# A delta-rule recurrence feeding a low-rank mixer and an MLP: the first group's product with w1 taken apart and moved into the recurrence

## The chip, the cores and the metric

The kernel runs on one core of one Trainium2 chip. The metric is device time in microseconds (us); the kernel before has a median of 610.22 us over three runs. A core has five engines that run their own instruction streams: PE (TensorE, matmuls; its weight loads are listed apart as PEld), DVE (VectorE), ACT (ScalarE), POOL (GpSimd) and SP (SyncE, which here only issues DMA transfers). SBUF is the on-chip memory of 128 partitions, PSUM the matmul output, 8 banks of 128 x 512 float32. PE's clock is granted by a throttle; the profile shows it as a share of full speed.

## The reference

Two blocks follow each other. The first is a delta-rule attention over B = 4 batches, H = 8 heads, S = 768 tokens, head size D = 48:

```
k_n = k / (|k| + 1e-6)
for t in range(768):                      # per batch and head, state is 48 x 48
    y[t]  = q[t] @ state
    state = state + beta[t] * outer(k_n[t], v[t] - k_n[t] @ state)
```

The eight heads side by side make x, 768 x 384 per batch. The second block mixes tokens by a product of rank 32 and then applies an MLP per token:

```
u   = x + (x.T @ U @ V).T                 # U 768 x 32, V 32 x 768
out = u + relu(u @ w1) @ w2               # w1 384 x 1536, w2 1536 x 384
```

q, k, v and beta are float32. U, V, w1 and w2 come as float64 and are made float32 on the chip.

## The kernel before, in words

**Attention.** Each batch is cut in 12 chunks of 64 tokens, and 6 chunks make a unit, so units 0 and 1 are batch 0, units 2 and 3 batch 1, and so on up to 7. For a unit the kernel loads k, q, v (and kz, a second copy of half of k) into one of two buffers `slot` (`load`, L301, issued on SP and POOL), normalises k, transposes k and q on PE (`grams`, L375), makes the products of k with itself and with q (L398), and inverts a triangular 64 x 64 matrix per chunk and head. The inversion (`blocks`) substitutes inside 32 x 32 blocks (or 16 x 16 ones) on DVE: `gs` (L450), `prod` (L459), `xt` (L460), and then a transpose into `zz` (L464). For units 0 to 2 the 16-blocks are joined into 32-blocks by two small products each, the joins: L503 (x of the block below), an ACT copy, L515, and DVE's add L519. For units 0 and 1 (`lone`) the operands lie alone on 64 partitions: `alone` is a part of the buffer `hs`, `parted` lies in `S1` and `S2`, written by `part` on ACT (L480), and each product uses the two diagonal tiles of 64 x 64, partitions 0 to 63 to rows 0 to 63 and 64 to 127 to 64 to 127. Two more products (L537 to L550) make the 64-blocks, and L619 and L624 prepare a unit for the recurrence.

**Recurrence.** `recur` goes chunk by chunk through a batch: b (product with the state, L673), z = v - b (DVE, L680), the state's increment (L690) and the new state s (DVE, L694). Outputs y are the products L597 and L604; ACT copies them into X (L587). `X` holds x of two batches. Batch 1 can't enter its recurrence before its own preparation is through; units are prepared two ahead.

**Mixer and MLP.** A batch's 768 tokens make three groups of 256. `front(b, i)` makes, for the first group of a batch, the token product `x.T @ U` (L929) and its copy `tt` (L932), then for each group the product with V (L944), adds it to x (L946), transposes u on PE (L960) and copies it (`ut`, L963). It waits for all 12 chunks of x. `wide(b, i)` has six `channels`, one for each pair of 128-wide feature tiles of w1 in `PAIRS`: six products of 128 x 128 by 128 x 256 (L1014), and ACT's relu into `hs` (L984). `add_up` makes sums (L1035, L1042) for the second product, which uses seven products of quarter size in the place of eight (`narrow`, L1102; results added to X by `gather`, L1048). A program on PE runs in a tiling mode: whole array, 64 x 64 quadrants, 32 x 32 tiles, or column strips of 32.

**Weights.** Fourteen slices come in: 0 is U, 1 is V, 2 to 7 the six pairs of w1, 8 to 13 w2. Each is a DMA of float64 into a staging place (L757, two DMAs of 384 KB from SP for a slice), three DVE instructions (L777, L783, L786) and one ACT cast (L763). There are three staging places, given per slice by `where`: 0 lies in the half of `X` that batch 1 will use, 1 is the buffer `wide`, 2 lies in `hs`. A slice waits for the one before it in its place, for the start of the slice before it, for unit 0's joins if it goes to `hs`, and all of them for `seeded`, a marker of unit 0's inversion.

**Order.** Each piece of work is a Python generator that yields one operation at a time. The order of the operations on all engines is one long list of numbers, ORDER; each entry lets one generator go a step further. `need(...)` names what a generator waits for before it is in the list's reach, and `emitted(...)` marks it as issued. Nothing is scheduled at run time: every engine executes its instructions strictly in this order, with waits on semaphores. The number behind a dot picks the PSUM slot: four pairs of banks (`pair`), of which the last is also the two `mix` banks used by the MLP, set aside by `reserve` from a point on. So an instruction that waits holds up all that stands behind it on its engine, and the DMA queues of SP and POOL are such streams too.

Of the kernel before, what the change touches and what calls it, by code (L numbers as in the profile page):

```python
# [14 lines left out]
L = 64  # L15
# [8 lines left out]
def kernel(ctx: ExitStack, tc: tile.TileContext, q: bass.AP, k: bass.AP, v: bass.AP, beta: bass.AP, moe_U: bass.AP, moe_V: bass.AP, moe_w_ch1: bass.AP, moe_w_ch2: bass.AP, out: bass.AP):  # L24
# [28 lines left out]
    1 0 1 0 1 0 1 0 22 1 38 22 38 22 21 22 14.0 21 2 21 37 151 21 20 151 15.1 36 2 36 167 26 166.2 36 167 26  # L53
    37 168.3 166 43 166 166 37 17.0 168 39 168 168 39 19 168 18.1 2 39 169 2.3 24 2 166 37 171.0 2 2 152 12 2
    168 171 43 153 170 12 36 39 29.2 168 166 38 24 12 172.3 166 171 153 24 173 19 3.1 38 24 3 172 174.0 23 3
    19 3 19 23 32.2 174 19 23 174 175 19 153 172 153 19 19 23 122 25 19 174 42 30.1 19 174 25 19 177 19 174 19
    174 178 19 19 179.2 19 19 3 19 33.3 179 184 40 183 35 183.0 181 186 40 179 187 40 41 122 183 179 187 42 41
    34 179 181.1 179 186 179 122 181 183 122 154 27 27 188 154 185.3 40 181 122 12 181.2 185 181 34 122 176.0
    181 155 181 34 155 181 183.1 122 180 122 180 183 189 27 176 34 180 181.2 183 181 185 180 176 181 180 181.3
    183 41 34 181 34 181 183 180 181 41 34 183.2 182 34 5.0 182 34 182 34 182 34 5.1 34 34 183 5 34 34 183 34  # L60
    5 183.3 34 183 182 4.0 183 182 183 4 190.2 34 156 6.1 190 156 190 6.0 194 192 195 4.3 122 6 195 194.2 122
    157 196 4 157 122 6 197.1 196 4.3 198 194 4 4.0 194 197 4 192.3 122 197 197 122 158 194.2 27 200 158 192
    122 122 194 192 159 159 199.0 194 4.1 192.3 4 122 194 201 4.1 122 199 122 192 199 199 194 160 202.2 122
    193 160 194.0 4 203 194 122 192 194 122 193 194.1 193 122 161 194 193 122 161 4.0 204 192 193 192 193 122
    194 192.3 192 191 4 194 122 191 122 192 4.0 191 206.1 4 191 202 205 4.3 191 191 4 52 207.0 202 4.3 202
    192.2 4 122 192 122 162 207 192 162 206 192 4.3 208 7.2 4 122 207 122 206 207 206 7.3 163 163 53 8.0 7 122
    53 7 122 209 4.1 210.2 4 122 4.3 8.1 4 164 164 122 4.3 122 54 8 210 4 53 211 212.3 4.0 210 4 210 122 4.0 8
    213.2 4 165 4.1 165 122 53 4 214 122 4.0 53 54 215.1 4 53 56 213 122 4.0 53 54 213 212 213 4 53 54 216 4.2
    212 212 217.0 54 4 216 4.3 54 215 4 54 218.2 122 215 4.3 215 54 216 219 217 4 46 218 217 122 217 46.1 216
    218 218 122 67 47.3 220 67 221 67 221 222 223.0 67 221 67 66 221 224.2 67 69 223 223 67 66 223 127.1 67 56  # L70
    224 223 224 66 224 51 224 69 66 66 66 69 49.3 127 66 50.0 225 66 62.2 44 55 226 44 123 55 127.1 228 55 44
    227.0 127 55 63.2 51 55 127.1 231 68 227 55 227 68 127 229.2 55 51 68 51 128.0 51 68 229 233 68 51 128 59
    68 233 51 55 229 68 51 59.1 244 51 56 60.0 245 51 68 234 246 51 56 51 51 128.2 51 234 128 51 51 51 235 249
    51 235 44 254 248.1 247.0 253 65 248 251 236 247 248 69 248 255 248 247 236 247 64 247 237 256 255 57 237
    57 257 251.2 64 251 253.1 251 255 253 64 253 238 57 57 238 64 64 64 240 258 64 259 64 240 259 64 259 64
    129.0 261 260 64 251.2 251 64 241 64 251 251 251 241 64 250 250 239 250 262 129 251.1 251 253.2 251 263
    253 64 251.0 251 64 251 242 250 253 253 251 250 253 250 252 242 264 64 252 252 64 252 64 253.1 253 9.2 64
    253 230.0 9 265 252 9.1 230 252 129.2 64 243 129 230 9 267 9.0 266.2 267 9 268q 266 64 266 9.1 64 268 9
    279.0 64 268 9.2 268 9 64 268 64 9.1 280 279 253.2 64 279 253 279 269 64 253 253 64 64 269 64 64 270 282
    64 64 270 9 78 286 271 287 284 288 283 271 288 283 288 283 272 289 285 283 272 285 273 290 285 285 273 275  # L80
    291 292 292 292 293 9.0 286.2 284.1 286 284 283 284 275 285 9 283 286 285 276 294 276 295 277 296 274 277
    297 298 286.1 284.0 298 286 284 265 284 278 284 286 286 299 281.2 9.0 300q 9 9.1 300 9 311.0 300 9.1 300 9
    300 9.1 312 281 9 301q 281 301 9.1 301 311 281 9 301 311 311 301 313.2 314 9.1 302q 9 9.0 302 9 315.1 302
    9.0 302 9 9.0 302 9 313 316 9.0 315 313 9 303 317 313 315 317 315 317 79 9.0 79 303 9 79 79 319 9.2 318.1
    9 232.0 79 80 79 80 9.2 232 304 79 80 232 9 79 80 9.0 80 82 320.2 9 318 80 9.0 318 304 9 72 318 80 80 72.0
    321 322 9.1 305 9 9.0 320 9 323.1 320 320 73.0 323 323 305 325 323 323 326 9.2 328.0 9 327 324.1 327 328
    9.2 307q 327 9 328 9.2 328 324 328 9 307 77 324 9.2 324 307 75.0 9 70 329.1 330 70 9.2 307 9 77 9.0 329
    307 329 9 329 77 9.2 333 9 334 76.0 306 335 81 308q 77 77 81 308 77 299 77 82 332.1 77 308 9.2 82 81 308 9
    77 82 337.0 77 9.2 308 9 77 9.2 332 338 9 339 337 332 77 332 309 337 77 337 92 77 92 70 130.2 77 92 92 77
    92 93 77 331.1 92 95 130 92 93 336.0 340 331 92 93 130.2 77 93 309 77 93 130 85 93 331 310 93 336 341 93  # L90
    336 341 77 81 130.2 95 77 85.1 95 130 342 88.0 77 342 81 343 86.2 77 81 355 89.1 81 77 357 94 131.0 77 359
    94 356.2 77 94 344q 131 356 94 344 77 94 360.1 344 356 94 356 344 77 360 81 356 77 344 77 362 131.0 77 345
    77 131 360 77 77 345 346 367 360 91 364 360 366 346 94 90 365 95 363 347 363 94 365 70 363 347 83 368 83
    370 361.2 365 83 364.0 365 369 366.1 364 90 366 363 348 366 364 90 361 365 348 365 361 363 369 349 371 369
    83 349 90 90 351 372 363 373 90 373 351 90 373 374 90 352 90 350 375 90 364.1 366.0 364 376 366 90 364 352
    366 90 364 90 366 90 10.2 132.1 10 377 10.0 358.2 10 132 10.0 353 90 10 358 358 353 380 90 90 354 381 90
    381 90 90 10.1 132q.0 10 382 379.2 124 132 10.1 90 383 90 124 383 124 10 90 394 378.0 90 10.1 378 379 384q
    10 379 124 378 90 379 10.1 384 10 90 395.0 384 10.2 124 384 10 90 384 90 10.1 396 395 124 385q 395 10 124
    395 90 10.2 385 124 10 124 397.1 90 385 10.0 385 10 90 10.2 90 385 10 398.0 399 90 397 124 10.2 90 397 386
    397 10 386 400 400 405 404 104 10.1 387 10 403 402 403 124 400 403 387 124 403 124 124 401 124 388 124 124  # L100
    124 406.2 10.1 398 10 388 398 407 398 10.1 404.0 10 404 402.1 404 402 406 402 10.0 406 390 10 406 408 106
    401 409 106 401 409 106 390 410 401 409 106 106 105 106 105 391 411 389 106 105 106 105 105 382 391 412
    108 105 401 105 101.1 413 403 414 401 402.0 402 105 404.2 404 404 102.1 402 392 107 402 107 98 404 107 416
    392 417 107 107 108 107 98.0 419 107 419 99.2 420 107 421 108 10.1 422.0 10 403 423.2 108 422 10.1 422 423
    422 393 10 423 422 423 423 425 424.1 10.0 425 426q 10 10.2 426 10 437.0 103 426 10.2 426 10 10.2 426 10 96
    424 438 96 10.2 437 424 427 437 96 437 10 424 103 10.0 415.2 10 103 103 439.1 10.0 415 427 415 10 103 428
    440 103 103 103 10.2 418.0 10 103 10.2 418 428 10 418 96 442 441.2 10.0 429q 443 10 429 443 10.0 103 429
    441 429 441 10 441 443 10.0 103 429 10 444.2 445 103 10.0 439 430 439 103 439 103 430 10 103 103 446 447.1
    10.0 103 431 10 103 10.0 444 103 10 447 444 444 431 103 447 447 103 118 448 133.0 103 118 118 103 118 449
    433q 118 121 103 118 121 449 433 133 118 119 103 118 119 133.2 433 103 119 433 449 119 133 433 111 119 103  # L110
    133q.1 119 450 451 111.0 103 133 119 103 434 452 119 103 121 103 103 103 112.2 453 103 114.1 455 434 460
    459 117 457 458 435 462 456 121 432 456 456 456 464 134.0 458 454.2 134 461.1 454 134q.0 454 461 454 458
    461 435 461 134 116 458 454 436 461 465 109 465 115.0 466 109 466 467 478 120 116 120 467 120 116 120 116
# [316 lines left out]
    def blocks(n):  # L430
# [45 lines left out]
        def part(h):  # L476
            to = parted(h).rearrange('p (r e) t -> p r e t', r=2)
            for y in range(2):
                yield op('act')
                nc.scalar.mul(to[:, :, :, BK * y:BK * y + BK], cut(zn, h), even[:, y:y + 1])  # L480
            emitted(('parted', n, h))
# [695 lines left out]
```

## Time and profile before

| | us |
|---|---|
| runs, three | 608.35, 610.22, 612.16 (median 610.22) |
| profiled execution, its own time | 612.87 |
| its span, first to last instruction | 611.2 |
| PE busy | 570.2 (93% of the span) |
| DVE busy | 388.7 (64%) |
| ACT busy | 232.1 (38%) |
| POOL busy | 97.8 (16%) |
| mean granted PE clock | 0.935 |
| last z of batch 0's recurrence (DVE, L680) | ends 110.9 |
| first transposes of unit 2's grams (PE, L375) | start 111.6 |
| substitution of units 0 to 3 through (DVE, L464) | 33.0, 57.8, 134.3, 178.9 |

How to read it: the profile is one execution. Busy time is that of an engine's own instructions; waits, semaphores and the issuing of DMAs are not counted. A group of instructions is named by its line in the program, engine, operation and operands, "out<-in". A float32 matmul leaves two records, except a transpose by the transposing form, so 36 products of 128 x 256 are 72 records. A share averaged over the span hides stages; the table of stretches gives the busy time in each of them.

### The profile page before, as it was taken

What the parts mean: (1) busy time and instruction counts of PE and PEld (TensorE: products, weight loads), DVE (VectorE), ACT (ScalarE), POOL (GpSimd) and SP (SyncE); (2) the same over time, 40 slices, a digit from 0 to 9 for tenths busy, and PEclk for the clock granted to TensorE, in tenths of its full rate; (3) what the DMA queues carried; (4) which work ended last, traced back from release to release, by engine and by line L of the source; (5) the groups of instructions that cost most, each with busy time, mean ns of one, the idle gap of its engine ahead of it and who ended that gap; (6) DMA issues with size and microseconds to landing.
All of it is one profiled execution on the core that took longest, in us unless ns stands there. A gap on an engine that the chain in (4) does not pass through costs nothing.

```text
span 611.2 us, 24520 instructions
## 1 busy us (share of the span) xinstructions
PE 570.2 (93%) x11070; PEld 485.8 (79%) x11070; DVE 388.7 (64%) x972; ACT 232.1 (38%) x495; POOL 97.8 (16%) x169
## 2 busy tenths in 40 slices
PE   5798975999899999999999999999999999999997
PEld 4688964788889778788979976988879768655997
DVE  4799855899992136999994299989722225132442
ACT  3546674642442335144234532632342231344000
POOL 8311050530101040512004204110010000000000
PEclk9955665799999999999999999999999999999999
DMA  9933658830000060720004305020000000000010
GB/s 146 155 89 116 203 154 174 136 78 8 4 16 1 29 95 3 137 72 17 15 4 97 82 3 96 8 66 3 29 3 2 29 4 1 26 1 1 17 36 27
DMA packets 63849, 33.34 MB, mean 55 GB/s; under 512 B 50816, under 2 KB 61824, under 8 KB 63744
## 3 DMA queue, kind: packets, MB, share of 16 engines
q1 hardware_dynamic: 56800, 23.21, 17.7%
q0 software_dynamic: 5344, 8.27, 6.3%
q8 instruction: 87, 1.43, 1.0%
q10 hardware_dynamic: 1600, 0.30, 0.3%
q14 instruction: 18, 0.15, 0.1%
HBM read 27.03 MB, written 4.72 MB: 52 GB/s over the span
## 4 chain that ended last, share of the span: by engine, by line
PE 63%; DVE 27%; issue 4%; ACT 3%; DMA 3%; ACTq 0%; DVEq 0%; SPq 0%
PE P L1102 21%; PE P L1014 10%; PE P L201 8%; PE P L838 7%; DVE xt L460 6%; DVE prod L459 6%; PE P L398 3%; PE P L375 2%; DMA wide<-in_moe_w_ch_dram 2%; PE P L604 1%; DVE gs L450 1%; PE P L649 1%; PE P L597 1%; DVE slot L417 1%; PE P L690 1%
## 5 line engine op out<-in xcount | busy, mean ns | idle before, releaser
L1014 PE MATMUL P<-ut,w_sb 128*128 128x256 f32 x456 | 106.3, 385 | 0.8 <-ACT hs L984 0.6
L1014 PEld LDWEIGHTS P<-ut,w_sb 128*128 128x128 f32 x456 | 84.1, 190 | 14.4 <-issue 1.8
L1102 PE MATMUL P<-w_sb,hs 128*128 128x192 f32 x456 | 79.3, 329 | 0.0
L1102 PEld LDWEIGHTS P<-w_sb,hs 128*128 128x128 f32 x456 | 74.0, 190 | 2.0 <-issue 0.6
L460 DVE TENSOR_TENSOR xt<-xt,prod 128x112 f32<-128x112 f32 (+21 forms) x200 | 64.6, 323 | 6.9
L1048 DVE TENSOR_TENSOR X<-X,P 128x192 f32<-128x192 f32 x85 | 29.5, 350 | 58.9 <-PE P L1102 55.6
L459 DVE TENSOR_TENSOR prod<-gs,xt 128x112 f32<-128x112 f32 (+21 forms) x200 | 63.9, 320 | 4.3
L984 ACT ACTIVATE hs<-P 128x512 f32<-128x512 f32 x54 | 32.1, 597 | 67.0 <-PE P L1014 46.6
L201 PE MATMUL P<-ut,w_sb 64*64 64x256 f32 x768 | 52.3, 385 | 1.6 <-ACT hs L984 1.3
L1102 PE MATMUL P<-w_sb,S 128*128 128x192 f32 x240 | 41.5, 327 | 1.3 <-DVE X L1048 1.3
L301 POOL DMA_DIRECT2D slot<-in_k_dram x44 | 29.2, 670 | 76.4 <-PE P L690 51.1
L1102 PEld LDWEIGHTS P<-w_sb,S 128*128 128x128 f32 x240 | 39.0, 190 | 2.1 <-DVE X L1048 2.0
L587 ACT COPY X<-P 64x192 f32<-64x192 f32 x96 | 30.0, 313 | 26.7 <-PE P L604 25.0
L563 ACT COPY slot<-zz 32x384 f32<-32x384 f32 x64 | 32.0, 508 | 16.7 <-DVE zz L519 13.7
L694 DVE TENSOR_TENSOR s<-s,P 128x192 f32<-128x192 f32 x40 | 13.9, 349 | 37.9 <-PE P L690 35.4
L375 PE MATMUL P<-ident,slot 128*128 128x128 f32 x192 | 31.6, 321 | 6.9 <-DMA slot<-in_k_dram 6.9
L398 PE MATMUL P<-slot 48*64 48x64 f32 x1536 | 33.7, 246 | 4.5 <-ACT slot L386 4.5
L398 PEld LDWEIGHTS P<-slot 48*64 48x64 f32 x1536 | 30.8, 158 | 8.6 <-ACT slot L386 6.0
L375 PEld LDWEIGHTS P<-ident,slot 128*128 128x128 f32 x192 | 26.5, 166 | 9.1 <-issue 7.2
L567 POOL MEMSET slot<- 32x384 f32 x32 | 13.3, 422 | 124.1 <-PE P L538 70.2
L838 PE MATMUL P<-slot,w_sb 128*128 128x384 f32 x96 | 33.1, 486 | 0.0
L201 PEld LDWEIGHTS P<-ut,w_sb 64*64 64x64 f32 x768 | 25.1, 133 | 8.9 <-ACT hs L984 2.3
(157 smaller groups left out, 975.5 us busy)
## 6 DMA issues: line engine op xcount, KB each, us to landing
out_dram<-X SPq DMA_DIRECT2D x22, 192.0 KB, 1.9
X<-in_moe_w_ch_dram SPq DMA_DIRECT2D x10, 384.0 KB, 4.1
wide<-in_moe_w_ch_dram SPq DMA_DIRECT2D x10, 384.0 KB, 4.5
slot<-in_k_dram SPq DMA_DIRECT2D x48, 72.0 KB, 4.7
slot<-in_k_dram POOLq DMA_DIRECT2D x44, 72.0 KB, 4.4
slot<-in_q_dram POOLq DMA_DIRECT2D x32, 72.0 KB, 5.1
slot<-in_q_dram SPq DMA_DIRECT2D x32, 72.0 KB, 5.0
slot<-in_v_dram SPq DMA_DIRECT2D x32, 72.0 KB, 2.8
```

The lines of the kernel that those rows point to most:

```text
L201: nc.tensor.matmul(to[half(g)], w[half(r), half(g)], x[half(r)], start=start, stop=stop, skip_group_check=True)
L375: nc.tensor.transpose(p_t[:, c // 3, c % 3], t[:, c, 2 * j:2 * j + 2].rearrange('p s d -> p (s d)'), ident)
L398: nc.tensor.matmul(p_g[half(g ^ par * i), par, c], kq[rows, c, j, 0, half(g)], kq[rows, c, j, i, half(g)], start=True, stop=True)
L459: nc.vector.tensor_tensor(out=prod, in0=gb[:, :, j:j + 1, j + 1:].to_broadcast([128, split, m, w]), in1=xb[:, :, 0:m, j:j + 1].to_broadcas ...
L460: nc.vector.tensor_tensor(out=xb[:, :, 0:m, j + 1:], in0=xb[:, :, 0:m, j + 1:], in1=prod, op=ALU.subtract)
L563: nc.scalar.copy(pg[quarter(i), :, at, :, a:a + BK], cut(zc, h)[quarter(i)].rearrange('p r (c j) t -> p r c j t', j=2))
L587: nc.scalar.copy(x[half(c % 2), c // 2, 4 * D * g:4 * D * (g + 1)].rearrange('p (j r d) -> p r j d', r=2, d=D), states(p_y)[half(g)])
L838: nc.tensor.matmul(to, w, t, start=start, stop=stop, skip_group_check=True)
L984: nc.scalar.activation(hs[:, fs[0]:fs[1] + 1:fs[1] - fs[0]], p_f, ACTF.Relu)
L1014: nc.tensor.matmul(p_f[:, x], w(x, t), ut[:, t], start=t == 0, stop=t == KT - 1)
L1048: nc.vector.tensor_tensor(out=to, in0=to, in1=p, op=ALU.add)
L1102: nc.tensor.matmul(to, of[0], of[1], start=of[2], stop=of[3], skip_group_check=True)
```

## The change

It has four parts. (1) For the first group of batch 0, relu(u @ w1) is taken apart: u = x + l with l of rank 32, so u @ w1 = x @ w1 + l @ w1. `early` transposes the x of the group's 256 tokens, which are chunks 0 to 3, before l is known; `ahead` multiplies it by w1 pair by pair and ACT keeps the sums, without relu, in `hs`. Once all of x is there, `low_rank` transposes tt, multiplies it by w1 in column strips, and `added` multiplies the result (32 rows per strip) by V; DVE adds this to what was kept, and `opened` applies relu. `front` of that group no longer transposes u, and its token product is in two steps. (2) The joins of units 0 and 1 use all four 64 x 64 tiles: the second half of the blocks goes to the other half of the output partitions, and `part` writes its operand to match, in three ACT instructions instead of one. (3) Waits: a unit's loads wait for the state of the unit two before it to be issued rather than for x; weight slices wait no longer for the start of the one before nor for `seeded`; the place in `hs` serves one slice, as soon as `alone` was read; the mix banks are set aside from chunk 3 of x on. (4) ORDER is another list.

```
-        yield need(('rec', n - 2), *[('x', b - 1, UC * hf + c) for c in range(UC)])
+        yield need(('rec', n - 2), ('state', n - 2))
...
             for y in range(2):
+                cols = slice(BK * y, BK * y + BK)
                 yield op('act')
-                nc.scalar.mul(to[:, :, :, BK * y:BK * y + BK], cut(zn, h), even[:, y:y + 1])
+                nc.scalar.mul(to[:, 0, :, cols], cut(zn, h)[:, 0], even[:, y:y + 1])
+                for g in range(2):
+                    yield op('act')
+                    nc.scalar.mul(to[half(1 - g), 1, :, cols], cut(zn, h)[half(g), 1], even[half(g), y:y + 1])
...
+                        to = half(rows.start // L ^ y // 6) if lone else rows
-                        nc.tensor.matmul(p_e[rows, y], of, zc[rows, e, SB:BK], start=True, stop=True)
+                        nc.tensor.matmul(p_e[to, y // 6, y % 6], of, zc[rows, e, SB:BK], start=True, stop=True)
...
-        where = [0, 1, 0, 1, 2, 0, 1, 2, 0, 1, 0, 1, 0, 1]
+        where = [0, 1, 0, 1, 2, 0, 1, 0, 1, 0, 1, 0, 1, 0]
...
-            yield need(('started', i - 1), ('freed', before), *[('joined', 0)] * (where[i] == 2))
+            yield need(('freed', before), *[('alone', 0, h) for h in range(2)] * (where[i] == 2))
...
-        yield need(('seeded', 0))
...
+    def early():
+        yield need(*[('x', 0, c) for c in range(4)])
...
+                nc.tensor.transpose(p_u[:, m, t], x[:, m, t * 128:(t + 1) * 128], ident)
...
+    def ahead(e):
...
+                nc.tensor.matmul(p_f[:, x], w1_sb[:, e, 256 * t + 128 * x:][:, 0:128], uts[0, 0][:, t], start=t == 0, stop=t == KT - 1)
...
+        nc.scalar.copy(hidden[:, fs[0]:fs[1] + 1:fs[1] - fs[0]], p_f)
...
+    def low_rank():
+        yield need(('sums of x', 0))
...
+            nc.tensor.transpose(p_a[:, t].rearrange('p g r -> p (g r)'), tt[half(0), 128 * t:128 * t + 128], ident[half(0), half(0)])
...
+                    nc.tensor.matmul(p_b[quarter(e % 4), 256 * y:256 * y + 256], at[:, t], w1_sb[:, e, 256 * t:256 * t + 256], start=t == 0, stop=t == KT - 1)
...
+    def added(k):
+        yield need(('low', k // 2))
...
+                nc.tensor.matmul(pair(o)[:, z, 256 * x:256 * x + 256], held[rows, 256 * (k // 2) + 128 * x:][:, 0:128], v_sb[rows, 0:GT], start=True, stop=True)
...
+            yield need(('kept', e))
+            yield op('dve')
+            nc.vector.tensor_tensor(out=at, in0=at, in1=pair(o)[:, z].rearrange('p (x n) -> p x n', x=2), op=ALU.add)
+            begin(opened(e, at))
...
     def reserve():
-        yield [('x', 0, NC - 2)]
+        yield [('x', 0, 3)]
```

In the new ORDER, 30 of the 36 products of `ahead` stand on PE between the first matmuls of batch 0's recurrence and its last; six stand behind it. On DVE the conversions of w1's first two pairs stand ahead of unit 1's substitution, and those of w2's last three slices between the z of the recurrence, as they did before. On SP the six loads of unit 2's k and q that it issues stand ahead of w2's fourth slice.

## The prediction

> **What bounds the kernel now.** I read the span in 40 slices first, then the busy time by stretches, then the waits and the chain inside the one stretch where no engine is full. The slices (each 15.3 us; digits are tenths):
>
> ```profile
> PE   5798975999899999999999999999999999999997
> DVE  4799855899992136999994299989722225132442
> PEclk9955665799999999999999999999999999999999
> ```
>
> PE, the matmul engine, is full from the eighth slice on. Before that it is not, and its clock is at half. DVE is at nine tenths in slices 9 to 12. In stretches (start:end, length, then busy time with the number of records for PE, PEld, DVE, ACT, POOL, then granted clock, DMA share, GB/s):
>
> ```profile
> 31.50:60.00 28.50, 25.73 (x749) 24.34 (x744) 26.87 (x71) 16.57 (x32) 5.13 (x9) 0.50 0.38 110
> 64.00:88.00 24.00, 21.76 (x709) 20.41 (x704) 18.67 (x34) 18.05 (x36) 5.97 (x9) 0.51 0.57 179
> 88.00:91.50 3.50, 1.17 (x71) 1.04 (x64) 0.51 (x2) 0.53 (x1) 3.11 (x6) 0.96 0.96 232
> 91.50:112.00 20.50, 12.46 (x386) 11.06 (x387) 12.24 (x27) 8.80 (x17) 0.54 (x1) 0.50 0.74 152
> 112.00:115.40 3.40, 3.40 (x52) 3.07 (x54) 3.26 (x6) 1.94 (x4) 3.40 (x7) 0.50 0.79 162
> 115.40:140.00 24.60, 24.40 (x398) 19.74 (x391) 22.91 (x59) 12.52 (x19) 10.32 (x16) 1.00 0.56 98
> 134.30:180.00 45.70, 43.67 (x1078) 38.66 (x1077) 42.78 (x106) 16.66 (x36) 3.22 (x6) 1.00 0.03 9
> 189.90:611.20 421.30, 409.58 (x7260) 342.31 (x7256) 239.21 (x601) 135.59 (x313) 48.55 (x83) 1.00 0.15 33
> ```
>
> The end of batch 0's recurrence (last z at 110.56, unit 2's grams from 111.6) splits the span. Behind it PE is busy 485.7 of 499.6 us: a PE microsecond removed there is one off the time, unless DVE, with 42.78 of 45.70 busy to 180, takes over. Ahead of it 12.46 of 20.5 us are busy. What PE and DVE wait for from 85 to 112 (waiter, releaser, total, times, longest):
>
> ```profile
> PE P L597 <- DVE z L680: 5.0, 1, 5.0
> PE P L690 <- DVE z L680: 3.3, 2, 3.2
> ...
> DVE power L777 <- DMA wide<-in_moe_w_ch_dram: 5.2, 1, 5.2
> DVE power L777 <- DMA X<-in_moe_w_ch_dram: 3.9, 1, 3.9
> ```
>
> DVE stands at a weight conversion whose slice hasn't landed; the z behind it is late, and PE with it. The chain says the same:
>
> ```profile
> 87.07 0.54 SPq L757
> 87.61 0.05 issue
> 87.70 10.84 DMA wide<-in_moe_w_ch_dram
> 98.57 0.05 DVEq L777
> 98.67 0.57 DVE power L777
> ```
>
> **Joins on four tiles** (before L503/L515, units 0 and 1). 96 records took 5.09 us at 35.1, half clock; the 384 of both units make 20.4 us. Two 64x64 tiles were used, now four. Least saving nothing, most half, 10.2; the nearest row, the same joins of unit 2 on four 32x32 tiles, passes 192 records in 1.8 us at full clock, 9 ns each against 53 at half clock here, so issue isn't the limit: I take half. parted costs 6 ACT copies by the 0.31 row instead of 2 of 0.61, 0.6 us more per half, beside x alone on PE. But DVE's order now has the conversions of w1 pairs 0 and 1 ahead of unit 1's substitution: the sum of its rows up to there is 28.2 against 26.2, so it ends 62 to 63 instead of 59.9. With joins of 5 us instead of 10 behind it, unit 1 is whole at about 74.5 against 77.4: of 10 us saved 3 reach the recurrence.
>
> **x w1 into the recurrence** (ahead). Of group (0,0)'s 36 products, 30 go between the recurrence's matmuls; two records of 0.220 us each (36 records in 7.93 us at 179.7), so 13.2 us at full clock, 26.4 at half. PE's own work from the last preparations to the recurrence's end was 13.4 us in 23.6. It begins 2 to 4 us earlier, at 84 to 86: 85 + 13.4 + 13.2 = 111.6, that is, the products fill PE's stalls if the clock is full. Dense products earn it: 91.5 to 112 at 12.46/20.5 had 0.50, 115.4 on had 1.00.
>
> The Trainium skill, "TensorE: Matmul & The Clock Gate", Part 1: full rate after a sustained busy window of some 3.4 us, half after an idle one. By that rule 31.5 to 60, at 25.73 of 28.50, would be full; the trace has 0.50 there, so the rule can't settle it by itself, and the small tiles may not count. By the rule the products cost the 13.2, by that row the 26.4.
>
> **Weights and loads.** The slices lose the waits for "started" and "seeded"; the q/k loads of unit 2 lose that for the x copies and now stand ahead of w2_3 on SP (six of 72 KB). Slices and loads shared the queues before (share 0.96 in 88 to 91.5, 10.84 us a slice). The slices that DVE waits for are then w2_3 at 99 to 101 (98.6 before), w2_4, and w2_5 at 109 to 110. z of chunks 7, 8 and 11 stand behind their conversions (2.1 us each) and PE's b and state behind z: last z 111 to 113. Both lanes give 111.6 to 113: **recurrence's end +1 us** (-4 by PE alone at the 2.36 us of an unimpeded chunk, +4 if a slice slips as the 10.84 did).
>
> **PE behind it.** Gone: 30 products, 30 x .44 = 13.2, and the transposes of u (front), 0.74; six products stay late. Added: 3 transposes 0.3; 18 products of tt by w1 in column strips, 36 records of 0.220 each; the token product's strips (L929) passed 24 records of 384 columns in 1.95 us, 0.081 each against 0.33 alone, so four run at once: 2.0, and 0.3 to 0.6 for mode changes and the odd strip, 2.3 to 2.6 (7.9 if none did); 12 rank-32 products of 128x256, 24 records: 5.3 at .44 each, 2.6 if row strips run two at once. No trace of before has a 32-row strip this wide; the nearest row, the 128x256 product, is the dear end, and I take it less a quarter, 4.0. Sum: -13.9 + 0.3 + 2.4 + 4.0 = **-7.2** (-8.6 to -5.7).
>
> The Trainium skill, "TensorEngine Tiling (Array Packing)", Key Properties: changing the tiling mode drains TensorE. The row behind it: six L1014 records between token products took 1.49 us instead of 1.32. Nine such blocks in the recurrence would be 1.5 us, by the rule and by the row; there PE still has slack, so the sum keeps it out.
>
> **PSUM.** The two mix banks are reserved from x of chunk 3 on, so the recurrence has three pairs of banks instead of four. Each of its four matmul groups a chunk holds one for about 0.7 us of matmuls and 0.36 of reading: 4.3 in 2.36 us, under two pairs. Nothing, at most one 0.36 read waited for in each of eight chunks, 3; the occupancy decides for nothing.
>
> **Clock at the seam.** Before, the 3.4 us from 112 ran at 0.50; if the products hold the clock, its grams run at full: 12 transposes 1.47 instead of 2.82 and others likewise: **-2** (0 to -2).
>
> **DVE behind it.** Six adds of 128x512 from PSUM (0.62 to 0.68, by the 0.553 row of 384) come between front and unit 3: 4 us; with what else moved past the seam the sum to the substitution of block 3 is 78.0 against 68.7 by rows, 73.3 against 64.5 in the trace's own pace. Before, DVE was ready for unit 3's join at about 182 and PE came at 189.87: 7 to 8 us of slack, the cover. Now DVE is ready 78 us behind the seam, PE arrives 73 to 76: a new stall of **+3.5** (0 to 8). That is what is late next.
>
> **Sum** against this execution (span 611.2, time 612.87): +1 - 7.2 - 2 + 3.5 = -4.7, span 606.5, time 608.2. The median shown, 610.22, lies 2.65 below the profiled one; so I give 605.5. 1% (6 us) is about what can be told from no change.
>
> **The rivals.**
> *Everything lands early* (0.22). The joins' 10 us arrive whole, since no conversion delays unit 1 where DVE waits for PE anyway, and the slices, without the waits, land ahead of z. For it: 3.9 and 5.2 us of waits to be had. Against it: q/k ahead of w2_3. Recurrence's end 5 earlier instead of 1 later, strips two at once -1.4: 605.5 - 6 - 1.4 = 598.
>
> *The clock stays at half in the recurrence* (0.21): the other side. The chain of z, b and state leaves gaps between products, the activity is that of 64 to 88, 0.51 with 90% busy, and 30 products cost 26.4 us on the path: 85 + 13.4 + 26.4 = 125 against 111.6. Then the seam's 2 isn't saved either: -7.2 + 13.2 = +6, DVE's stall mostly gone: 610.2 + 6 = 616. It decides from a mean clock below 0.75 in 85 to 112: the products then cost 17.6, 4.4 more than the stalls hold, and the forecast's gain is gone. Against it: 0.96 right behind 64 to 88, and L1014's form at 1.00 wherever it runs.
>
> *DVE swallows it* (0.12). The order past the seam is DVE's sum, 9.3 us more by rows, and a stall of 8 instead of 3.5: 610.
>
> The change does what it says in each of these; that the work isn't moved at all is excluded by the instructions' order.
>
> **How the numbers follow.** Forecast 0.45, between 600 and 610.5: two fifths of it below 604.1, the rest within 1%. Faster: 0.18 + 0.22 = 0.40. Within: 0.27 + 0.10 = 0.37. Slower (over 616.3 or near it): 0.21 + 0.02 = 0.23. Its own range being 600 to 610.5, the two outer cases stretch it to 595 and 617: what is left out is half of the slow case, which can reach 620, and the far end of the early one.
>
> **What would show it.** Joins of units 0 and 1: 96 records in 2.6 us. Clock 85 to 112 above 0.9 and the new products at 0.22 a record: forecast; 0.44: the slow case. Last z between 108 and 115. Rank-32 products at 0.11 or 0.22 a record. PE waiting 0 to 8 us for DVE ahead of unit 3's join. PE behind the seam busy about 478 instead of 485.7. Wrong above all if the seam moves by more than 5 us, through clock or slices, since all behind it shifts with it.

## The result

The changed kernel takes 606.43 us (median of 20 runs, 602.87 to 610.89), the kernel before 610.74 us beside it (20 runs, 607.48 to 615.76). The ratio is 0.9929, with a 95% interval from 0.9908 to 0.9951: 4.3 us, 0.7% faster. Forecast were 605.5 us and 4.7 us less. The profiled execution of the changed kernel took 605.11 us and has a span of 603.4 us, against 612.87 and 611.2 before, so the two profiles lie 7.8 us apart where the medians lie 4.3 apart; part of that is the opening, below.

In the new program the line numbers are others. The product of x by w1 kept for later is L972 (ACT's copy of it L978), the transposes of tt L990, their product with w1 L1005, the rank-32 products L1019, DVE's additions L1027; the recurrence has z at L698, state products at L708, outputs at L615 and L622; grams are L378 and L401, the joins L519 and L533, DVE's transpose at the end of a substitution L467, weight conversions L798, products of w1 and w2 L1142 and L1230.

The 40 slices of the changed kernel's page (15.1 us each):

```profile
PE   5566799999999999999999999999999999999997
DVE  4899755899896229999983699898413226132542
PEclk9957569998999999999999999999999999999999
```

PE is now full, and its clock high, from the sixth or seventh slice on instead of the eighth. The stretches (columns as before: start:end, length, busy time and records of PE, PEld, DVE, ACT, POOL, then granted clock, DMA share, GB/s):

```profile
31.50:60.00 28.50, 19.44 (x758) 17.59 (x760) 27.00 (x66) 19.93 (x41) 4.53 (x8) 0.62 0.49 134
64.00:88.00 24.00, 19.74 (x637) 17.73 (x638) 15.71 (x31) 20.23 (x40) 7.04 (x11) 0.53 0.62 165
88.00:91.50 3.50, 3.50 (x73) 2.91 (x75) 0.31 (x2) 1.55 (x2) 1.70 (x4) 1.00 1.19 202
91.50:112.00 20.50, 20.02 (x480) 16.21 (x471) 13.42 (x27) 11.14 (x22) 3.22 (x5) 1.00 0.60 142
112.00:115.40 3.40, 3.30 (x112) 2.23 (x114) 3.04 (x6) 2.88 (x6) 3.34 (x6) 1.00 1.15 171
...
110.68:603.40 492.72, 478.48 (x8714) 400.04 (x8709) 310.43 (x776) 171.91 (x382) 64.03 (x108) 1.00 0.16 34
...
141.00:144.00 3.00, 1.78 (x191) 1.72 (x192) 2.96 (x6) 0.32 (x1) 0.98 (x1) 1.00 0.02 5
144.00:147.40 3.40, 3.40 (x34) 3.37 (x22) 3.37 (x9) 1.95 (x4) 0.00 (x0) 0.59 0.00 0
```

From 91.5 to 112 PE is busy 20.02 us instead of 12.46, at clock 1.00 instead of 0.50, and yet the recurrence ends at about the same place. I mark its end by the block of twelve of unit 2's transposes right behind it, which starts at 110.68 (111.58 before); six more records of them, 0.7 us, stand inside the recurrence now, at 103.62. Behind that point PE is busy 478.48 of 492.72 us; the row of the kernel before is

```profile
111.58:611.20 499.62, 485.68 (x8722) 408.05 (x8718) 308.02 (x770) 170.92 (x380) 65.32 (x110) 1.00 0.16 34
```

The last two rows of the table show something new: a thin stretch at unit 2's joins, in which PE is busy for little more than half of the time, and half clock in the 3.4 us behind it. What PE, and then DVE, wait for from 85 to 112 in the changed kernel:

```profile
PE P L622 <- DVE z L698: 0.2, 1, 0.2
```

```profile
DVE z L698 <- PE P L691: 4.5, 4, 3.3
DVE power L798 <- DMA X<-in_moe_w_ch_dram: 4.4, 1, 4.4
DVE power L798 <- DMA wide<-in_moe_w_ch_dram: 1.5, 1, 1.5
```

PE's 8.3 us of waits for z are gone but for 0.2. DVE still waits 5.9 us for weight slices, and now it waits for PE too. The times by section, from the two profiles (the end of a substitution is the end of DVE's transpose L464, now L467; the times 33.0, 57.8, 134.3 and 178.9 in the table of the kernel before are where these transposes start):

| section | before | changed | difference |
|---|---|---|---|
| start to the end of unit 0's substitution | 35.04 | 32.74 | -2.3 |
| from there to the end of unit 1's substitution | 24.82 | 26.55 | +1.7 |
| from there to the end of the recurrence | 51.72 | 51.39 | -0.3 |
| from there to the end of the span | 499.62 | 492.72 | -6.9 |

The added instructions on PE, from the timeline (start, length, engine, line, operands, records):

```profile
121.53 1.50 PE L1005 MATMUL P<-w_sb,ut 128*32 128x256 f32 x24
122.96 0.88 PE L378 MATMUL P<-ident,slot 128*128 128x128 f32 x6
123.76 1.13 PE L1019 MATMUL P<-v_sb,ut 32*128 32x256 f32 x8
124.83 0.87 PE L378 MATMUL P<-ident,slot 128*128 128x128 f32 x6
125.63 1.49 PE L1005 MATMUL P<-w_sb,ut 128*32 128x256 f32 x12
```

24 records on four column strips take 1.43 us until the next group starts, 0.06 each; 12 records on two strips take 1.42, 0.12 each. Eight rank-32 records on two row strips take 1.07, 0.13 each, where a product on the whole array takes 0.22.

### The profile page after: what moved, and what is told of

It is laid out like the page before. It is cut to its first block, busy times and chain, and to the rows that moved or that the text cites. A ratio compares the mean times of both kernels' runs of the same rounds, so it can differ in the third digit from the quotient of the medians.

```text
span 603.4 us, 24671 instructions
## 1 busy us (share of the span) xinstructions
PE 560.4 (93%) x11133; PEld 471.2 (78%) x11133; DVE 391.5 (65%) x979; ACT 244.1 (40%) x520; POOL 98.0 (16%) x169
## 3 DMA queue, kind: packets, MB, share of 16 engines
q8 instruction: 87, 1.43, 1.0%
## 5 line engine op out<-in xcount | busy, mean ns | idle before, releaser
L1142 PE MATMUL P<-ut,w_sb 128*128 128x256 f32 x384 | 88.7, 384 | 0.3 <-ACT hs L1112 0.2
L1142 PEld LDWEIGHTS P<-ut,w_sb 128*128 128x128 f32 x384 | 71.1, 190 | 11.9 <-issue 1.8
L1230 PE MATMUL P<-w_sb,hs 128*128 128x192 f32 x456 | 79.5, 329 | 0.2 <-DVE X L1176 0.2
L1230 PEld LDWEIGHTS P<-w_sb,hs 128*128 128x128 f32 x456 | 73.9, 190 | 2.0 <-DVE X L1176 0.6
L1112 ACT ACTIVATE hs<-P 128x512 f32<-128x512 f32 x48 | 28.7, 597 | 72.0 <-PE P L1142 53.7
L1230 PE MATMUL P<-w_sb,S 128*128 128x192 f32 x240 | 43.3, 337 | 0.7 <-DVE X L1176 0.7
L1230 PEld LDWEIGHTS P<-w_sb,S 128*128 128x128 f32 x240 | 40.3, 195 | 1.6 <-DVE X L1176 1.4
L401 PE MATMUL P<-slot 48*64 48x64 f32 x1536 | 30.8, 232 | 4.6 <-ACT slot L389 4.4
L401 PEld LDWEIGHTS P<-slot 48*64 48x64 f32 x1536 | 28.0, 146 | 8.6 <-ACT slot L389 5.7
L378 PE MATMUL P<-ident,slot 128*128 128x128 f32 x192 | 27.2, 294 | 6.8 <-DMA slot<-in_k_dram 6.8
L1230 PE MATMUL P<-w_sb,slot 128*128 128x192 f32 x180 | 30.4, 327 | 0.9 <-DVE X L1176 0.9
```

The source lines that it names most:

```text
L401: nc.tensor.matmul(p_g[half(g ^ par * i), par, c], kq[rows, c, j, 0, half(g)], kq[rows, c, j, i, half(g)], start=True, stop=True)
L1112: nc.scalar.activation(hs[:, fs[0]:fs[1] + 1:fs[1] - fs[0]], p_f, ACTF.Relu)
L1142: nc.tensor.matmul(p_f[:, x], w(x, t), ut[:, t], start=t == 0, stop=t == KT - 1)
L1230: nc.tensor.matmul(to, of[0], of[1], start=of[2], stop=of[3], skip_group_check=True)
```

## The experiments

Each kernel ran beside the kernel before. Where two changed kernels are compared, the difference is that of their ratios to the kernel before.

**The products in another place.** The 30 tokens of `ahead` that stood inside the recurrence, and ACT's five copies, are moved in ORDER to just ahead of the last pair's.

```
 ORDER: ... [142 x7, 143 x7, 144 x7, 145 x7, 146 x7 between the recurrence's tokens] ... 147 ...
     -> ... [the recurrence's tokens alone] ... 142 x7 143 x7 144 x7 145 x7 146 x7 147 ...
```

> The changed kernel with one thing undone: the 30 products of x by w1 (and ACT's five copies of their sums) stand behind the end of batch 0's recurrence instead of inside it; same work, another place. My theory: inside they filled PE's stalls and held its clock. Then the recurrence ends no earlier than 107 (110.7 with the products), its clock from 92 to 107 falls back to about 0.5, and the 13.2 us come on top behind it: 10 to 15 us slower than the changed kernel, some 617 to 621, 1% slower than the kernel before or more. Rival: PE is a full queue in the recurrence too and the place is the same to it: the recurrence ends 10 to 13 us earlier, near 98, and the time is within 3 us of the changed kernel.

Measured: 620.14 us, ratio to the kernel before 1.0191 (1.0167 to 1.0216), 16 us slower than the changed kernel, 1 us more than expected. Its stretches:

```profile
88.00:91.50 3.50, 1.73 (x93) 1.56 (x92) 2.15 (x5) 1.72 (x2) 2.23 (x4) 0.94 1.23 160
91.50:100.00 8.50, 0.49 (x18) 0.33 (x13) 2.15 (x4) 1.59 (x3) 0.00 (x0) 0.50 1.00 227
100.00:112.00 12.00, 9.92 (x288) 8.87 (x290) 8.74 (x19) 5.55 (x12) 2.24 (x3) 0.50 0.32 90
112.00:115.40 3.40, 3.40 (x31) 3.26 (x28) 3.26 (x5) 1.50 (x4) 2.93 (x6) 0.57 1.09 190
112.35:618.20 505.85, 490.63 (x8773) 411.25 (x8769) 309.63 (x776) 174.88 (x387) 63.72 (x107) 1.00 0.15 33
```

The recurrence ends at 112.35, later than with the products in it, and what is behind takes 505.85 us, 13.1 more than 492.72. That is about the 13.2 us of products, though other things differ there too and about cancel: the seam, the 3.4 us right behind the recurrence, runs at 0.57 here, and the half clock at unit 2's joins doesn't occur. From 91.5 to 100 PE has next to nothing to do, because DVE waits 7.7 us for one slice, and the clock, 0.94 in 88 to 91.5, is at 0.50 from there on. So the products cost the recurrence nothing, and with them the clock stays where it already was ahead of them. As a plain undo the kernel is hard on the change: the 30 products stand in one block, and DVE, which has 22.90 us to do from 115.4 to 140 in the changed kernel, does 9.03 there.

**The products left out.** The step further: 26 of them aren't executed anywhere.

```
+                if e == 5 or (e < 2 and t == 0):
-                nc.tensor.matmul(p_f[:, x], w1_sb[...], uts[0, 0][:, t], start=t == 0, stop=t == KT - 1)
+                    nc.tensor.matmul(p_f[:, x], w1_sb[...], uts[0, 0][:, t], start=t == 0, stop=t == KT - 1 or e < 2)
```

> The changed kernel with 26 of the 30 products inside the recurrence left out and not made up for (the first group's hidden layer is then wrong): 11.4 us less work on PE at full clock, 22.9 at half. My theory: the products fill waits and hold the clock. Without them the slices and a half clock set the recurrence's end, near 112 as in the kernel with the products late; behind it the first transposes run at half clock again. So 0 to 4 us slower than the changed kernel, for 11.4 us less work. Rival (PE is simply full there and each product costs its time): recurrence's end near 99, 8 to 11 us faster.

Measured: 612.8 us, ratio 1.0042 (1.0017 to 1.0067). With 11.4 us less work on PE it is 7 us slower than the changed kernel, more than my theory's 4. The profile:

```profile
91.50:112.00 20.50, 10.91 (x340) 9.14 (x331) 11.55 (x23) 9.47 (x18) 2.12 (x5) 0.65 0.71 157
112.00:115.40 3.40, 3.12 (x69) 2.89 (x70) 2.49 (x5) 2.23 (x5) 3.19 (x5) 0.50 0.66 129
114.43:612.50 498.07, 481.88 (x8713) 402.95 (x8709) 310.39 (x776) 171.89 (x382) 63.55 (x107) 0.99 0.16 34
```

The recurrence ends at 114.43; this profile's opening was late, so the fair figure is from the end of unit 0's substitution, 78.5 us against 77.9. So leaving 11.4 us of work out brought the end no nearer. The loss is behind it, 498.07 against 492.72, with the same work there, and 5.2 of these 5.3 us are there by the end of unit 3's substitution (83.15 us behind the recurrence against 77.99). In that stretch PE is busy 78.60 us against 75.56, at a mean clock of 0.94 against 0.98: 3.0 us go with the clock, 1.8 of them by the half clock until 118, the rest with a thin stretch and half clock from 148 on. PE's idle time is 4.55 against 2.43; the 2.1 us are two waits of 1.2 and 1.0 us which the profile gives as issue, that is, for nothing that it shows, so their cause stays open. This is one execution, and its mean clock, 0.958, is above that of the kernel's other eleven (0.930 to 0.940); the 7 us are the median of all twelve.

**Useless work in their place.** The products late as in the first experiment, and in each of the 30 places a product that nothing reads.

```
+            if token == 'fill':
+                nc.tensor.matmul(P[:, 6, 0:128], ident, ident, start=True, stop=True)
+                continue
```

> As the kernel with the products behind the recurrence, and in each of the 30 places inside it a product of 128x128 by 128 columns that nothing reads: half a product's columns, 2 records of 0.11 us at full clock, 6.6 us in all, useless work added. My theory (dense products hold the clock): granted clock near 1.0 from 88 to the recurrence's end, which is no later than without the useless work, between 103 and 108, and the time is 0 to 5 us below that of the kernel with the products late and no filling. Rival (the clock comes from elsewhere, products are only cost): same clock as without filling, the recurrence's end and the time 4 to 8 us later.

Measured: 621.67 us, ratio 1.0223 (1.0192 to 1.0254). The clock is 0.95 from 91.5 to 100, 0.75 to 112 and 1.00 in the 3.4 us behind (0.50, 0.50 and 0.57 without filling). The recurrence ends at 113.0, not between 103 and 108. So both expectations were half right: dense work does raise the clock there, at 0 to 1.5 us for 6.6 us of work, but a higher clock by itself brings the end no nearer. Something else set it. Nor did the full clock at the seam shorten what is behind: unit 2's substitution ends 44.34 us behind the recurrence instead of 45.58, but the whole takes 506.10 us instead of 505.85. Half clock at unit 2's joins, 0.63 for 3.4 us, occurs here and didn't without filling.

**The slices left out.** The DMAs of w2's last three slices aren't issued, once in the changed kernel and once with the products late.

```
                 yield op(e)
-                queue.dma_start(out=to, in_=of)
+                if i < 11:
+                    queue.dma_start(out=to, in_=of)
```

> The changed kernel without the transfers of w2's last three slices (six DMAs of 384 KB; the conversions run on what lies in their places, so the second MLP product is wrong): DVE and z never wait for them. Theory A (PE, full at full clock with the products, bounds the recurrence as much as the slices): end of the recurrence 108 to 110, 1 to 3 us faster than the changed kernel. Theory B (the slices alone set it): end of the recurrence near 103, 6 to 8 us faster.

> The kernel with the 30 products behind the recurrence, without those three slices' transfers too. There the end of the recurrence was at 112.4 with PE busy 0.5 of 8.5 us from 91.5 to 100. Theory (without the products the slices alone set the recurrence's end): it comes to 99 to 103, 9 to 13 us earlier, and the time falls by about as much, to some 608 to 611. Rival (the chain of z, b and state on a half clock sets it): it comes no earlier than 108, and the time falls by less than 4.

Measured: in the changed kernel 606.07 us, ratio 0.9931 (0.9896 to 0.9966), and the recurrence's end at 109.16. That is theory A's place for the end, without the 1 to 3 us that it put on the time: nothing was gained. With the products late 615.58 us, ratio 1.0076 (1.0047 to 1.0104) against 1.0191, 7 us, and the recurrence's end at 106.6 instead of 112.35: between the two expectations. So without the products the slices hold the end back by about 6 us (6.9 from the end of unit 0's substitution); that the rest is the chain of z, b and state, at clocks of 0.50 to 0.60, is my reading and not tested. With the products in it PE is full and, by the median, the slices don't matter. In single executions they can: in the profile of the kernel without DVE's additions, below, DVE waits 7.1 us for the first of these three slices, ACT's copy L646 stands behind that slice's cast, PE waits 2.4 us for the copy, and the recurrence ends at 113.95. The change has put PE's work where the slices made it wait, up to the point where both limits lie at about the same place.

**The slice ahead of the loads.** Of the six transfers of unit 2's q and k on SP, all go behind w2's fourth slice.

```
 ORDER: ... 54 54 53 54 53 53 (unit 2's q, k) ... 134 134 (the slice) ...
     -> ... 134 134 54 54 53 54 53 53 ...
```

> The changed kernel with the six transfers of unit 2's q and k that stood on SP ahead of w2's fourth slice moved behind it. My theory: in the recurrence PE is full at full clock (20.0 of 20.5 us from 91.5), so DVE's 4.4 us wait for that slice isn't on the path: end of the recurrence and time within 1 us of the changed kernel. Rival: the slice holds up z and with it the recurrence: 3 to 4 us faster.

Measured: 605.84 us, ratio 0.9932 (0.9905 to 0.9958): no difference in the time, as expected. The slice did come earlier (DVE takes it at 92.75 instead of 97.11), but the recurrence ended at 112.1, not within 1 us: the next slice was taken at 101.28 instead of 100.68, after a wait of 2.2 us, PE waited 1.6 us for the z behind it, and the clock from 100 to 112 was 0.86.

**The joins on two tiles.** The order is kept, only the tiles and ACT's operand are as before.

```
-                        to = half(rows.start // L ^ y // 6) if lone else rows
+                        to = rows
```

> The changed kernel with the joins of units 0 and 1 on the two diagonal tiles again and ACT's operand written in one instruction as before; all else as changed. The joins of a half then take 5.1 us on PE instead of 2.7, 10 us more in all. My theory: DVE's substitution stands in front of them and PE waits there, so the recurrence ends 2 to 4 us later, the time is 608 to 611. Rival: the joins are the chain that the end of the recurrence hangs on, and their 10 us are the change's gain: 8 to 10 us later, 614 to 617.

> The joins of units 0 and 1 on two tiles once more, since the first time gave no profile that can be read: time as the first time, 1.000 of the kernel before. Theory: the joins' second half of PE time moves the end of the recurrence 2 to 4 us (to 112 to 114 from 109.7 to 110.7), and nothing changes behind it. Rival: the end of the recurrence stays within 1 us and the 4 us come from elsewhere.

Measured: 609.41 us, ratio 1.0002 (0.9972 to 1.0032), and 609.62 us, ratio 0.9995 (0.9962 to 1.0027), 4.4 and 4.0 us slower than the changed kernel. Only the second has a profile that can be read. In it the recurrence ends at 113.89 (110.68 in the changed kernel's first profile, 109.69 in its second). Part of that is the opening: from the end of unit 0's substitution it is 80.4 us against 77.9 and 77.7. What is behind takes 494.61, 1.8 to 1.9 more, where nothing was expected: 1.2 of it by the end of unit 3's substitution, with a wait of PE of 0.9 us at unit 2's joins that the profile gives as issue. So 10 us of PE time in the joins are worth some 2.5 at the recurrence's end, nearer to the 2 to 4 expected than to the rival's 8 to 10. The whole 4 us are of the size of the whole gain: with two tiles the rest of the change comes to no difference from the kernel before.

**DVE's additions twice, and not at all.**

```
+            nc.vector.tensor_tensor(out=at, in0=at, in1=pair(o)[:, z]..., op=ALU.add)
             nc.vector.tensor_tensor(out=at, in0=at, in1=pair(o)[:, z]..., op=ALU.add)
```

> The changed kernel with each of DVE's six additions of 128x512 from PSUM made twice (the low-rank term counts double in the first group): 6 x 0.68 = 4.1 us more on DVE between the end of the recurrence and unit 3's joins. In the changed kernel PE waited 0.8 us for DVE there, so DVE has no slack left. My theory: 3 to 4 us slower, about 610. Rival (DVE's work there is hidden, the slack of 7 us that the kernel before had is still there): within 1 us.

> The changed kernel without the six additions (the low-rank term is left out of the first group's hidden layer): 4.1 us less on DVE. My theory: PE waits only 0.8 us for DVE, so 0 to 1 us faster. Rival (DVE is the bound of this stretch and swallowed some of the gain): 3 to 4 us faster.

Measured: twice 610.08 us, ratio 1.0009 (0.999 to 1.0027), 5 us slower for 4.1 us of work; not at all 605.28 us, ratio 0.9927 (0.9898 to 0.9956), no difference. The two longest of PE's waits in the kernel with the additions twice, from the recurrence's end to unit 3's joins (the first isn't there in the changed kernel):

```profile
PE P L401 <- DVE hs L1028: 2.4, 3, 1.0
PE P L1231 <- DVE X L1177: 0.7, 1, 0.7
```

And the longest of DVE's in the kernel without them:

```profile
DVE S L1162 <- ACT hs L1031: 3.0, 1, 3.0
```

With them gone DVE waits 3.0 us for the relu behind PE's low-rank products. Its profile has the recurrence's end late, for the slice named above, and behind it 492.15 us against 492.72. DVE and PE are balanced in this stretch: what is added to DVE is paid in full, what is taken from it alone is worth nothing that can be told at an interval of 2 us to either side.

**The thin stretch filled.** Six products of the second MLP product go between unit 2's first two joins.

```
 ORDER: ... 265.1 265 (L533) 267 244 (six products L1230) ...
     -> ... 244 265.1 265 267 ...
```

> The changed kernel as it is, a second time, for the comparison with the next ones on one chip and for a second profile. Theory: time 0.993 of the kernel before; the end of the recurrence differs from profile to profile by the landing of w2's last slices, and the time with it. Rival: the end of the recurrence is the same to 1 us, and the spread of the times comes from behind it.

> The changed kernel with one group of PE's instructions moved: six products of the second MLP product (12 records, 1.3 us) that stood behind the first two joins of unit 2 now stand between them, where PE waits 0.43 us for ACT; nothing else moves on any engine. In the changed kernel's profile PE is busy 1.78 of 3 us there (141 to 144) and the granted clock is at half for the next 3.4 us, in which 1.3 us of such products took 3.8 with their waits. Theory: that dip is the cost of a thin stretch, and goes: 1 to 2.5 us faster than the changed kernel. Rival: DVE, whose inversion of unit 2 ends late, sets this place; the join comes 0.9 us later and nothing is gained, 0 to 1 us slower.

Measured: the changed kernel again 605.39 us, ratio 0.9922 (0.9895 to 0.9949), its recurrence ending at 109.69; with the six products moved 608.03 us, ratio 0.9939 (0.9906 to 0.9972). Of the 1.0 us between the recurrence's ends in the changed kernel's two profiles, 0.7 lie in the opening. In the kernel with the six products moved the half clock is gone (1.00 from 144.5 to 151) and those products took 2.22 us instead of 3.79, and nothing was gained: unit 3's substitution ends 78.1 us behind the recurrence, 78.0 in the changed kernel, as the rival had it. But the one profile doesn't show that the six products kept the clock up. From 135 to 150 the changed kernel, this one and the one without the three slices have

```profile
135.00:150.00 15.00, 13.76 (x411) 12.63 (x410) 14.59 (x32) 5.13 (x10) 0.98 (x1) 0.89 0.01 4
135.00:150.00 15.00, 14.12 (x459) 13.12 (x454) 14.13 (x34) 5.17 (x9) 0.98 (x1) 1.00 0.02 4
135.00:150.00 15.00, 13.72 (x424) 12.13 (x414) 14.45 (x34) 4.37 (x10) 1.52 (x3) 1.00 0.02 5
```

and the last has the thin stretch unfilled, PE busy 1.77 of 3 us, with clock 1.00 behind it. So has the kernel with the products late. In the eight other profiles with such a stretch the clock behind it is 0.50 to 0.63; what decides is open. Where the clock stayed up by itself, without the slices, unit 3's substitution ended 76.8 us behind the recurrence, 1.2 us sooner: that is about what the half clock costs, and moving the six products into the joins, which come later for it, didn't earn it.

The opening accounts for part of what differs between executions. The end of unit 0's substitution lies at 31.9 to 33.0 us in eight of twelve profiles with the new order, at 33.5 and 34.0 in two, and at 35.9 and 36.3 in two. The latter two belong to executions of 614.17 and 609.48 us, slower than their kernels' medians. DVE's waits from 14 us to that point, in the kernel before, then in the changed kernel (in the one with the products left out they come to 4.3 us):

```profile
DVE slot L405 <- ACT slot L402: 1.6, 1, 1.6
DVE betas L331 <- ACT beta_rows L328: 1.0, 1, 1.0
DVE slot L417 <- PE P L398: 0.9, 1, 0.9
```

```profile
DVE betas L334 <- ACT beta_rows L331: 0.7, 1, 0.7
```

Of the kernel before there is one profile only (35.04), so how much of the 2.3 us is the new order and how much the execution is left open.

## Why the prediction was right, point by point

**The time** was right to a microsecond (-4.7 forecast, -4.3 measured), and the forecast's case is the one that came: PE's work behind the recurrence shrank, the recurrence's end hardly moved. Not every term was, and that the total agrees to 0.4 us is in part luck: the recurrence's end was put 1.9 us too late and DVE's stall 3.2 us too long, and between the two profiles the difference is 7.8.

**Joins.** Half the PE time was right: 96 records of L533 take 2.72 us (2.6 foreseen). That 3 of the 10 us reach the recurrence's end was close, 2.5 by the undo without the opening. The working had unit 1's substitution end at 62 to 63; it ended at 59.29. The 2 us of conversions ahead of it are there (+1.7 in the second section); what failed is that the step left out the opening, where DVE's waits went from 3.5 to 0.7 us.

**x w1 into the recurrence.** "The products fill PE's stalls if the clock is full" is what the first, second and fourth experiments show. The clock was 1.00 from 88 to 112, the forecast's condition; with the products late it was 0.50 from 91.5, the rival's. The sum behind it came out for another reason than it gave: its 13.4 us of PE's own work are what the kernel before shows at a clock of 0.57 (13.2 of 23.58 us from 88 on), and were added to products priced at full clock. PE is busy 26.20 of the 26.68 us from 84 to 110.68 now, 13.0 besides the products, because two more blocks of preparation (83.77 to 86.51, at half clock) and six of unit 2's transposes lie in it. That is luck. The two rows on which I set the condition don't say what earns a clock: 31.5 to 60 is 0.62 with 19.44 of 28.5 busy (758 records), the kernel before has 0.50 with 25.73 (749 records). The busy share isn't the measure. The cost of a change of tiling mode, which the sum kept out, may be there in a full PE: six products take 2.79 us from 96.17 to the next group's start at 98.96, 0.15 more than 12 records of 0.22. The Trainium skill, "TensorE: Matmul & The Clock Gate", Part 1, ties the rate to how busy PE was in a short window; the fall to 0.50 in the kernel with the products late, where PE stands idle from 91.5, agrees; 25.73 of 28.50 busy at 0.50 doesn't, if busy is the profile's busy.

**Weights and loads.** "Both lanes give 111.6 to 113" was the right picture, with an end 1 to 3 us too late for the changed kernel, 110.68 and 109.69 in two profiles, for the opening's sake. With the products late it is 112.35, the slices' lane; with them in place it is PE's lane in most profiles, and leaving the slices out brings 109.16.

**PE behind it.** The forecast was -7.2, and PE is busy 7.2 us less. That agreement is partly luck. Column strips took 2.85 us (2.4 foreseen, the second group using only two strips), rank-32 products 3 x 1.07 = 3.2 (4.0), the transposes of tt 0.33: with the 13.94 that went, -7.6. The six transposes of unit 2 that now stand in the recurrence, which the forecast left out, take another 0.7 away. The seam gave 1.7, half of the 3.4 us at 0.50 before (2 foreseen, as a term of its own). Against these stand 1.7 lost in the half clock behind unit 2's joins, and 1.1 that I can't place.

**DVE behind it** is the step that failed as a term: +3.5, measured +0.3 (PE's idle time behind the recurrence is 14.24, 13.94 before). That DVE would be ready 78 us behind the end was exact, 78.0; PE didn't come at 73 to 76 but with it. PE had lost the difference on the way, 0.8 us waiting at unit 2's joins and 1.7 in the half clock behind them among it. So the lost slack was real, as the additions made twice show (+5), but it was a balance, not a stall, and it cost 0.3 us of waiting where 3.5 were put. With the recurrence's end 1.9 earlier than forecast, that makes the 7.8 between these two profiles. That the medians differ by 4.3 is because the profile before is of an execution 2.1 us above its median and that after of one 1.3 below; a sum made against one execution can't be better than that.

**The rivals.** Nothing landed early: with the slices left out altogether the end came at 109. The half clock didn't stay, and the experiment with the products late shows the half clock there as soon as the products are gone. DVE swallowed nothing that taking the additions away would give back. The result lies in the range, and within 1% as the larger part of the forecast's own case had it.

**Not tested.** The waits of part (3) and the earlier reservation of the mix banks were taken back in no experiment, so what they give alone isn't known.

## What to carry to other kernels

When one engine waits for transfers in one stage and is the bound in the next, work moved from the second into the first can be free, down to the point where the waits are used up; the measure of it is the same work left out, which here made the kernel slower. Work that fills waits can also keep the matmul clock up for what follows, so a stretch is priced with the clock that its neighbours leave it; but what it wins can be lost further on, as the 1.2 us were that the useless work won. Where two engines are both at nine tenths, an edit that loads one of them is paid in full and one that relieves only one of them buys nothing.

## What was not expected

Taking away 11.4 us of work cost 7 us. A higher mean clock didn't go with a shorter time. The two executions of the changed kernel with the highest, 0.975 and 0.978, took 609.94 and 610.26 us, above its median of 606.43, and with the joins on two tiles two with 0.997 took 614.36 and 613.51 (median 609.62); none of these has a profile, so the cause is open. In the same way the profiled execution of the kernel with the products left out had clock 1.00 from 31.5 to 60, where the changed kernel's had 0.62, and unit 1's substitution took the same 26.6 us behind unit 0's, since DVE (26.95 and 27.00 of 28.5 us busy) sets that stretch. And a light stretch of 3 us at unit 2's joins, PE busy 1.78, was followed by 3.4 us at clock 0.59 in the middle of a part where PE otherwise runs at 1.00, in most of the profiles but not in all.
